# Attention and squared-ReLU FFN: softmax sums of four head pairs in one group, their inverse spread by DMAs from 16 rows

## The chip, the cores and the metric

The kernel runs on one core of one Trainium2 chip. The metric is device time in microseconds. Three runs of the kernel before took 481.18, 482.60 and 482.84 us, median 482.6.

The core has engines that work side by side, each with its own queue of instructions: TensorE (PE; PEld is its weight load), VectorE (DVE), ScalarE (ACT), GpSimd (POOL) and SyncE (SP). The last two only issue DMAs here, apart from some set-up on GpSimd. An instruction that waits holds up what is behind it on its own engine.

## The reference

Linear attention with projected keys and values, and then a feed-forward layer with a squared ReLU:

```python
k_proj = np.einsum('ks,bhsd->bhkd', E, k)
v_proj = np.einsum('ks,bhsd->bhkd', F, v)
scores = scale * np.matmul(q, k_proj.transpose(0, 1, 3, 2))
scores = scores - np.max(scores, axis=-1, keepdims=True)
attn = np.exp(scores)
attn = attn / (np.sum(attn, axis=-1, keepdims=True) + 1e-09)
attn_out = np.matmul(attn, v_proj)
x = attn_out.transpose(0, 2, 1, 3).reshape(B * S, H * D)
h = np.maximum(x @ w_in, 0.0)
out = h * h @ w_out
```

There are 8 batches (B), 8 heads (H), 1024 tokens (S) of 64 values (D), 64 projected keys, 512 columns in x, 2048 in h.

## The kernel before, in words

**Units.** A batch's attention is one `Attention` object. Its eight heads are four pairs, `pr` 0 to 3. The feed-forward layer of a batch is cut into two `Chunk`s of 512 tokens. After a start on plain products, both products of the layer use a seven-product scheme on 2x2 blocks (Strassen's, with sums of blocks formed on VectorE): `Group.p1` to `p7` for the first product, `second_spread` for the second. `sum_x` forms the block sums of x, four VectorE operations each.

**Attention of one batch, as steps of the plan.**
- `load_kv` and `load_q` bring K, V and Q from HBM by DMAs that GpSimd issues and that cast to bf16. Each of the three has one buffer, so the next batch's K and V wait for `project` to have read this one's.
- `project` multiplies K and V by E and F on TensorE; VectorE and ScalarE copy the result out of PSUM. `transpose_k_dma` and `transpose_q_dma` transpose by DMA, issued on SP.
- `scores(pr)` is four 64x64 matmuls into a PSUM tile `ps_att` of two banks, then one Exp on ScalarE into a tile `expT` (four buffers).
- `sums_spread(pr)` serves two pairs. Eight matmuls with a 64x32 block of ones put the sum of every token into 32 equal rows of `ps_att`, for each of four (pair, head) places. ScalarE makes the inverse as Exp(-Ln(sum)) in `inv`. SP then issues eight DMAs, each from 32 rows to 32 rows of a tile `rs`, so that every head has its inverse on all 64 rows. `inv` and `rs` share three buffers.
- `values(pr)` is four 64x64 matmuls from `expT` and the projected values into `ps_att`; two VectorE multiplications by `rs` (L409) write xT, the input of the feed-forward layer.

Batch 1 has another form, `sums(pr)`: the inverse is made twice by ScalarE, once for each pair, and four VectorE copies (L373) fill the missing rows.

**PSUM.** Up to batch 2's scores there are two `ps_att` tiles in turn (`turn["pairs"]`), from then on one. Every group of the attention therefore waits until the group before it has been read out. Four banks serve the first product, two the second.

**Order.** TensorE's order is that of the program, written by hand (`manual_schedule`). On the other engines a scheduler orders the instructions by its own simulation of when they become ready. The program is a generator: each `yield` is a step, and `plan` holds what `at(step, ...)` or `on(step, batch, name)` puts behind a step. In the steady part, `both()` takes in each step one block of the first product and mostly one block of the second, eight matmuls of 128x128 by 256 columns. A loop over b from 1 to 6 places, with t = 56 (b - 1), the attention of batches b + 1 and b + 2 among these steps; 56 steps are two chunks. For batch b + 2, `project` is at t + 30, `transpose_k_dma` at t + 32, the next K and V at t + 34, scores at 44, 47, 53 and, in the next period, 1; sums at 50 and 3; values at 7, 10, 20, 23 of the next period. In those steps, `second_spread` hands out an output (`put`) at steps 9, 21, 25, 29, 37, 49, 53 and 57 of the period. An output tile `o_sb` (three buffers) is stored by a DMA on SP. `keep` copies a partial product out of PSUM into a tile `u` (five buffers) that a later `relu_sum` (L666) or `put` adds.

The start differs: batch 0 runs in small pieces while the weights arrive, batch 1's attention lies among steps 36 to 60 of the next stretch, and batch 2's scores and first sums among the 16 steps of `chunk[1, 0].first_plain()`.

Of the kernel before, what the change touches and what calls it, by code (L numbers as in the profile page):

```python
# [9 lines left out]
P = 128  # L10
F32 = mybir.dt.float32
BF16 = mybir.dt.bfloat16
AF = mybir.ActivationFunctionType
# [6 lines left out]
def kernel(  # L20
# [43 lines left out]
    part_pool = ctx.enter_context(tc.tile_pool(name="part", bufs=5))  # L64
    out_pool = ctx.enter_context(tc.tile_pool(name="outp", bufs=3))
# [54 lines left out]
    nc.vector.memset(ones[:], 1.0)  # L120

# [100 lines left out]
    class Attention:  # L222
# [134 lines left out]
        def sums(self, pr):  # L357

            ps = att_psum()
            for j in range(2):  # L360
                for o, par, a, r in VALUE_QUADS:
                    c = 32 * (2 * a + j)
                    nc.tensor.matmul(
                        ps[c:c + 32, par], lhsT=ones[r, 0:32], rhs=self.e[pr + j][r, par], start=True, stop=True
                    )
            rs = [soft_pool.tile([P, 2, TCH], F32, tag="rs", name="rs") for _ in range(2)]
            nc.scalar.activation(rs[1][:], ps[:], AF.Ln)
            nc.scalar.activation(rs[0][:], rs[1][:], AF.Exp, scale=-1.0)
            nc.scalar.activation(rs[1][:], rs[1][:], AF.Exp, scale=-1.0)
            for j in range(2):  # L370
                for a in range(2):
                    have, lack = 32 * (2 * a + j), 32 * (2 * a + 1 - j)
                    nc.vector.tensor_copy(rs[j][lack:lack + 32], rs[j][have:have + 32])  # L373
                self.rs[pr + j] = rs[j]

        def sums_spread(self, pr):

            ps = att_psum()
            for j in range(2):
                for o, par, a, r in VALUE_QUADS:  # L380
                    c = 32 * (2 * a + j)
                    nc.tensor.matmul(
                        ps[c:c + 32, par], lhsT=ones[r, 0:32], rhs=self.e[pr + j][r, par], start=True, stop=True
                    )
            inv = soft_pool.tile([P, 2, TCH], F32, tag="rs", name="inv")
            nc.scalar.activation(inv[:], ps[:], AF.Ln)
            nc.scalar.activation(inv[:], inv[:], AF.Exp, scale=-1.0)
            for j in range(2):
                rs = soft_pool.tile([P, 2, TCH], F32, tag="rs", name="rs")
                for a in range(2):  # L390
                    have = 32 * (2 * a + j)
                    for to in (64 * a, 64 * a + 32):
                        nc.sync.dma_start(rs[to:to + 32], inv[have:have + 32])
                self.rs[pr + j] = rs
# [43 lines left out]
    class Chunk:  # L438
# [103 lines left out]
        def keep(self, ps):  # L542
            u = part_pool.tile([P, DM], F32, name="u")
            nc.scalar.copy(u[:], ps)  # L544
            return u
# [97 lines left out]
    class Group:  # L643
# [35 lines left out]
        def p5(self):  # L679
            self.other = bank(n=turn["bank"] + 2)  # L680
            self.product(5, self.other, True)
            self.kept5 = self.chunk.keep(self.other[:])

        def p6(self):
            self.product(6, self.chain)
            self.u2 = self.chunk.keep(self.chain[:])
# [21 lines left out]
    with tc.manual_schedule(engines={PE}):  # L708
# [81 lines left out]
        at(45, nxt.sums, 0)  # L790
        at(47, nxt.scores, 2)
        at(49, nxt.scores, 3)
        at(50, nxt.values, 0)
        at(52, nxt.values, 1)
        at(53, nxt.sums, 2)
# [11 lines left out]
        at(1, nxt.transpose_k)  # L807
        at(3, nxt.scores, 0)
        at(5, nxt.scores, 1)
        at(7, nxt.sums_spread, 0)  # L810
        at(9, nxt.scores, 2)
        at(11, nxt.scores, 3)
        turn["pairs"] = 1
        run_all(chunk[1, 0].first_plain())
# [45 lines left out]
        def on(step, b, name, *args):  # L860
            at(step, lambda: getattr(atts[b], name)(*args))

        for b in range(1, B - 1):
            t = 56 * (b - 1)
            if b > 1:
                on(t + 1, b + 1, "scores", 3)
            on(t + 3, b + 1, "sums_spread", 2)
            on(t + 7, b + 1, "values", 0)
            on(t + 10, b + 1, "values", 1)
            on(t + 20, b + 1, "values", 2)  # L870
            on(t + 23, b + 1, "values", 3)
            for c in range(2):
                at(t + 24, lambda b=b, c=c: chunk[b + 1, c].sum_x())
            if b + 2 < B:
                on(t + 2, b + 2, "transpose_q_dma")
                if b + 3 < B:
                    at(t + 2, begin, b + 3)
                    on(t + 3, b + 3, "load_q")
                on(t + 30, b + 2, "project")
                on(t + 32, b + 2, "transpose_k_dma")  # L880
                if b + 3 < B:
                    on(t + 34, b + 3, "load_kv")
                on(t + 44, b + 2, "scores", 0)
                on(t + 47, b + 2, "scores", 1)
                on(t + 50, b + 2, "sums_spread", 0)
                on(t + 53, b + 2, "scores", 2)
# [34 lines left out]
```

## Time and profile before

| what | value |
|---|---|
| median of three runs | 482.6 us |
| profiled execution, its own time | 482.35 us |
| span of the instructions in it | 480.5 us |
| TensorE busy | 470.4 us (98%) |
| VectorE busy | 350.7 us (73%) |
| ScalarE busy | 287.2 us (60%) |
| DMA of `rs` from `inv` on SP | 96 of 128 KB |
| small matmuls of `sums_spread` (L382) | 96, 4.9 us busy |
| Ln and Exp of `sums_spread` (L386, L387) | 12 each, 12.3 and 12.8 us busy |
| multiplications of `values` (L409) | 56, 36.0 us busy, 684 ns each |
| K and V, 1024 KB each in SBUF, issue to landing (median) | 9.5 and 15.8 us |

The profile is of one execution, whose span starts with its first instruction. Times in it are in microseconds unless ns is given. "Busy" is the union of an engine's instructions. A group line names the source line, the engine, the operation, what it writes and reads, the shapes and the count; behind the bar come busy time, mean ns of one, and the idle time of the engine just before, with what ended it. In a timeline, the first two columns are start and duration; brackets give the idle time before and what ended it. "issue" is time in which the engine waited for nothing that the profile shows. In the page's strips each digit is a fortieth of the span, in tenths.

### The profile page before, as it was taken

The numbers are of one execution on the slowest core, as the hardware profiler recorded it, in microseconds if no ns is written. First come the engines' busy times: TensorE is split into PE (matmuls) and PEld (weight loads), VectorE is DVE, ScalarE is ACT, GpSimd is POOL, SyncE is SP. The second block draws the span as 40 slices with busy tenths as digits, with TensorE's granted clock in tenths as the row PEclk, the third lists the DMA queues.
The fourth block names the chain that finished last, engine by engine and source line by source line (L and its number), as shares of the span: only waits on it lengthen the run. The fifth ranks groups of instructions, "written<-read, shape, count | busy, mean of one in ns | idle before, by whom it ended". The sixth has DMA issues, their size and how long they took to land.

```text
span 480.5 us, 10027 instructions
## 1 busy us (share of the span) xinstructions
PE 470.4 (98%) x4106; PEld 351.5 (73%) x4106; DVE 350.7 (73%) x613; ACT 287.2 (60%) x466; POOL 32.4 (7%) x45
## 2 busy tenths in 40 slices
PE   8999999999999999999999999999999999999996
PEld 3444445537878788787878778887887778888885
DVE  2456897956996679767897579966797678967671
ACT  2464467397547774678546785477745775565641
POOL 7310010200010000100010000100000000000000
PEclk9999999999999999999999999999999999999999
DMA  9999998999949496767939499495811054101012
GB/s 184 204 205 206 221 164 150 168 230 189 197 86 168 122 201 163 119 134 186 196 103 182 93 220 175 96 160 139 203 56 55 23 132 111 67 23 67 24 65 89
DMA packets 80046, 66.98 MB, mean 139 GB/s; under 512 B 30720, under 2 KB 76032, under 8 KB 80000
## 3 DMA queue, kind: packets, MB, share of 16 engines
q0 software_dynamic: 30640, 29.23, 39.4%
q1 hardware_dynamic: 49216, 36.97, 29.2%
q8 instruction: 32, 0.52, 0.4%
q10 hardware_dynamic: 144, 0.13, 0.1%
q14 instruction: 14, 0.11, 0.1%
HBM read 59.24 MB, written 16.78 MB: 158 GB/s over the span
## 4 chain that ended last, share of the span: by engine, by line
PE 71%; DVE 22%; ACT 3%; issue 2%; DMA 1%; DVEq 0%; ACTq 0%
PE ps_bank L652 28%; PE ps_second L572 27%; PE ps_bank L489 6%; DVE h L150 3%; DVE x_sum L150 3%; DVE h L666 3%; DVE s L150 2%; PE ps_att L329 2%; DVE xT L409 2%; PE ps_second L549 2%; PE ps_att L405 2%; DVE kp L246 1%; DVE rs L373 1%; DVE kp L247 1%; DVE w_in_sum L150 1%
## 5 line engine op out<-in xcount | busy, mean ns | idle before, releaser
L150 DVE TENSOR_TENSOR h<-h 128x1024 bf16<-128x1024 bf16 (+1 forms) x182 | 108.0, 616 | 39.1 <-ACT h L662 25.4
L652 PE MATMUL ps_bank<-x_sum,w_in_sum 128*128 128x256 bf16 x624 | 93.9, 273 | 0.0
L652 PEld LDWEIGHTS <-w_in_sum 128*128 128x128 bf16 x832 | 78.7, 98 | 16.2 <-issue 7.5
L572 PEld LDWEIGHTS <-h 128*128 128x128 bf16 x832 | 80.8, 98 | 10.6 <-DVE h L150 0.2
L662 ACT ACTIVATE h<-ps_bank 128x512 bf16<-128x512 f32 x104 | 62.9, 605 | 28.5 <-PE ps_bank L652 28.3
L544 ACT COPY u<-ps_bank 128x512 f32<-128x512 f32 x107 | 63.2, 591 | 26.6 <-PE ps_bank L652 23.6
L666 DVE CUSTOM_DVE_ANT_0 h<-ps_bank,u 128x512 bf16<-128x512 f32 x104 | 68.9, 685 | 13.0 <-PE ps_bank L652 12.5
L652 PEld LDWEIGHTS <-w_in 128*128 128x128 bf16 x624 | 58.8, 98 | 16.2 <-issue 9.5
L677 ACT COPY ps_bank<-ps_bank 128x512 f32<-128x512 f32 x52 | 29.7, 570 | 66.1 <-PE ps_bank L652 66.1
L572 PEld LDWEIGHTS <-s 128*128 128x128 bf16 x624 | 61.0, 98 | 7.1
L652 PE MATMUL ps_bank<-xT,w_in 128*128 128x256 bf16 x416 | 62.5, 273 | 0.0
L572 PE MATMUL ps_second<-w_out_sum,s 128*128 128x256 bf16 x416 | 62.4, 273 | 0.0
L572 PE MATMUL ps_second<-w_out_sum,h 128*128 128x256 bf16 x416 | 62.2, 273 | 0.0
L572 PE MATMUL ps_second<-w_out,h 128*128 128x256 bf16 x416 | 60.3, 273 | 0.0
L409 DVE TENSOR_TENSOR xT<-ps_att,rs 128x512 bf16<-128x512 f32 x56 | 36.0, 684 | 15.9 <-PE ps_att L405 15.9
L489 PE MATMUL ps_bank<-xT,w_in 128*128 128x512 bf16 x192 | 45.3, 379 | 1.8 <-DVE xT L434 1.0
L485 ACT ACTIVATE h<-ps_bank 128x512 bf16<-128x512 f32 x48 | 28.1, 606 | 16.1 <-PE ps_bank L489 15.9
L150 DVE TENSOR_TENSOR o_sb<-ps_second,u 128x512 f32<-128x512 f32 x27 | 18.5, 684 | 25.9 <-PE ps_second L572 20.7
L489 PEld LDWEIGHTS <-w_in 128*128 128x128 bf16 x192 | 17.7, 98 | 24.6 <-issue 6.2
L343 ACT ACTIVATE expT<-ps_att 128x1024 bf16<-128x1024 f32 x32 | 32.9, 1036 | 2.9 <-PE ps_att L329 2.5
L652 PE MATMUL ps_bank<-x_sum,w_in 128*128 128x256 bf16 x208 | 31.4, 273 | 1.4 <-DVE h L666 1.4
L652 PE MATMUL ps_bank<-xT,w_in_sum 128*128 128x256 bf16 x208 | 31.3, 273 | 0.0
(104 smaller groups left out, 477.2 us busy)
## 6 DMA issues: line engine op xcount, KB each, us to landing
out_dram<-o_sb SPq DMA_DIRECT2D x63, 256.0 KB, 2.4
rs<-inv SPq DMA_DIRECT2D x96, 128.0 KB, 2.8
K_sb<-in_k_dram POOLq DMA_DIRECT2D x7, 1024.0 KB, 9.5
V_sb<-in_v_dram POOLq DMA_DIRECT2D x7, 1024.0 KB, 15.8
Q_sb<-in_q_dram POOLq DMA_DIRECT2D x7, 1024.0 KB, 12.6
w_out<-in_moe_w_out_dram POOLq DMA_DIRECT2D x4, 512.0 KB, 17.9
w_in<-in_moe_w_in_dram POOLq DMA_DIRECT2D x3, 512.0 KB, 15.0
k_f<-in_k_dram SPq DMA_DIRECT2D x1, 512.0 KB, 4.9
```

The source lines that it names most:

```text
L150: return nc.vector.tensor_tensor(out=o, in0=x, in1=y, op=op)
L329: nc.tensor.matmul(ps[o, par], lhsT=self.kT[r, h % 4, h // 4, :], rhs=self.qT[r, h, n, :], start=True, stop=True)
L343: nc.scalar.activation(e[:], ps[:], AF.Exp, scale=SCALE)
L409: nc.vector.tensor_tensor(out=self.xT[:, pr, :, par], in0=ps_x[par].rearrange("p (c t) -> p c t", c=2), in1=rs[:, par].rearrange("p (c t) ...
L485: nc.scalar.activation(h, ps.rearrange("p (a t) -> p a t", a=2), AF.Relu)
L489: nc.tensor.matmul(ps[:], lhsT=w_in_blk(cb, fb), rhs=self.xT[:, cb, self.c].rearrange("p a t -> p (a t)"), start=(cb == 0), stop=(cb == NC ...
L544: nc.scalar.copy(u[:], ps)
L572: nc.tensor.matmul(ps[:, i * HM:(i + 1) * HM], lhsT=self.h_form(n, fb)[:, i * P:(i + 1) * P], rhs=w_out_form(n, fb), start=fresh and i == ...
L652: nc.tensor.matmul(ps[:, j * HC:(j + 1) * HC], lhsT=w_in_form(n, cb, 2 * self.g + j), rhs=self.chunk.x_form(n, cb), start=fresh and j == 0 ...
L662: nc.scalar.activation(self.out(kh, a), ps[:], AF.Relu)
L666: nc.vector._custom_dve(TENSOR_ADD_SAT, out=self.out(kh, a), in0=ps[:], in1=more[:], s0=3.0e38, s1=0.0)
L677: nc.scalar.copy(self.chain[:], self.first[:])
```

## The change

- `sums_all` replaces the two `sums_spread` of a batch, from batch 2 on. Sixteen matmuls accumulate in two rounds, m = 0 and 1, into one `ps_att`. Their weights are `pick`: 32 columns, of which 16 are ones and 16 zeros, so that pair 2m + j lands in 16 rows of a 32-row block and the other round adds zeros there. There is one Ln and one Exp for four pairs (`inverse_of`), in a tile `inv` with a buffer of its own.
- `spread` issues four DMAs for a pair, each from 16 rows to 64: a source row is read four times. All 16 DMAs of a batch are placed behind the sums, in one step. Four `rs` tiles share three buffers, `inv` is no longer among them.
- Batch 1's first sums (`sums(0, True)`) use the same DMAs instead of a second Exp and four copies; its second sums keep their form. Its later steps move by one.
- Batch 2's `transpose_k` and first two scores move one step later; its sums come at step 13 of `first_plain` instead of 7 and, for the second half, step 3 of the steady part.
- In the steady part `project` moves from 30 to 49 (24 for batch 3), with the transposition and the next K and V a step behind it; scores to 37, 40, 43, 46; all sums and spreads to 53; values to 6, 9, 19, 22 of the next period (7, 10, 19, 22 for batch 2); `sum_x` to 23 and 33 instead of twice 24; `transpose_q_dma` from 2 to 12, `load_q` from 3 to 26.
- The tiles of `keep` have two buffers for the first product and two for the second instead of five in common, `o_sb` has two instead of three.

```diff
-    part_pool = ctx.enter_context(tc.tile_pool(name="part", bufs=5))
-    out_pool = ctx.enter_context(tc.tile_pool(name="outp", bufs=3))
+    part_pool = ctx.enter_context(tc.tile_pool(name="part", bufs=2))
+    out_pool = ctx.enter_context(tc.tile_pool(name="outp", bufs=2))
...
+    pick = const_pool.tile([P, 2, 32], BF16, name="pick")
+    nc.vector.memset(pick[:], 0.0)
+    for m in range(2):
+        nc.vector.memset(pick[:, m, 16 * m:16 * m + 16], 1.0)
...
+            if by_dma:
+                self.inverse_of(ps)
+                for j in range(2):
+                    self.spread_rows(pr + j, {(par, a): (32 * (2 * a + j), par) for o, par, a, r in VALUE_QUADS})
+                return
...
+        def sums_all(self):
+            ps = att_psum()
+            for m in range(2):
+                for j in range(2):
+                    for o, par, a, r in VALUE_QUADS:
+                        c = 32 * (2 * j + par)
+                        nc.tensor.matmul(
+                            ps[c:c + 32, 0 if r == LO else 1], lhsT=pick[r, m], rhs=self.e[2 * m + j][r, par],
+                            start=m == 0, stop=m == 1, skip_group_check=True,
+                        )
+            self.inverse_of(ps)
+
+        def inverse_of(self, ps):
+            self.inv = soft_pool.tile([P, 2, TCH], F32, tag="inv", name="inv", bufs=1)
+            nc.scalar.activation(self.inv[:], ps[:], AF.Ln)
+            nc.scalar.activation(self.inv[:], self.inv[:], AF.Exp, scale=-1.0)
+
+        def spread(self, pr):
+            m, j = divmod(pr, 2)
+            self.spread_rows(pr, {
+                (par, a): (32 * (2 * j + par) + 16 * m, 0 if r == LO else 1) for o, par, a, r in VALUE_QUADS
+            })
+
+        def spread_rows(self, pr, at):
+            rs = soft_pool.tile([P, 2, TCH], F32, tag="rs", name="rs")
+            for o, par, a, r in VALUE_QUADS:
+                row, n = at[par, a]
+                nc.sync.dma_start(rs[o, par], self.inv[row:row + 16, n].unsqueeze(1).broadcast_to((16, 4, TCH)))
+            self.rs[pr] = rs
...
-        def keep(self, ps):
-            u = part_pool.tile([P, DM], F32, name="u")
+        def keep(self, ps, tag="second"):
+            u = part_pool.tile([P, DM], F32, name="u", tag=tag)
...
-        at(45, nxt.sums, 0)
...
+        at(45, nxt.sums, 0, True)
...
-        at(7, nxt.sums_spread, 0)
...
+        on(13, 2, "sums_all")
+        for pr in range(4):
+            on(13, 2, "spread", pr)
...
+        def project(step, b):
+            on(step, b, "project")
+            on(step + 1, b, "transpose_k_dma")
+            if b + 1 < B:
+                at(step + 1, begin, b + 1)
+                on(step + 1, b + 1, "load_kv")
+
+        project(24, 3)
         for b in range(1, B - 1):
             t = 56 * (b - 1)
...
-            on(t + 7, b + 1, "values", 0)
-            on(t + 10, b + 1, "values", 1)
-            on(t + 20, b + 1, "values", 2)
-            on(t + 23, b + 1, "values", 3)
+            for pr, step in enumerate((7, 10, 19, 22) if b == 1 else (6, 9, 19, 22)):
+                on(t + step, b + 1, "values", pr)
             for c in range(2):
-                at(t + 24, lambda b=b, c=c: chunk[b + 1, c].sum_x())
+                at(t + 23 + 10 * c, lambda b=b, c=c: chunk[b + 1, c].sum_x())
             if b + 2 < B:
-                on(t + 2, b + 2, "transpose_q_dma")
+                on(t + 12, b + 2, "transpose_q_dma")
                 if b + 3 < B:
-                    at(t + 2, begin, b + 3)
-                    on(t + 3, b + 3, "load_q")
-                on(t + 30, b + 2, "project")
-                on(t + 32, b + 2, "transpose_k_dma")
-                if b + 3 < B:
-                    on(t + 34, b + 3, "load_kv")
-                on(t + 44, b + 2, "scores", 0)
-                on(t + 47, b + 2, "scores", 1)
-                on(t + 50, b + 2, "sums_spread", 0)
-                on(t + 53, b + 2, "scores", 2)
+                    on(t + 26, b + 3, "load_q")
+                    project(t + 49, b + 3)
+                for pr in range(4):
+                    on(t + 37 + 3 * pr, b + 2, "scores", pr)
+                on(t + 53, b + 2, "sums_all")
+                for pr in range(4):
+                    on(t + 53, b + 2, "spread", pr)
```

## The prediction

> **What bounds the kernel now.** I read the page first, then busy time by period, the waits of TensorE, and the timeline around one group of softmax sums.
>
> ```profile
> span 480.5 us, 10027 instructions
> ...
> PE 470.4 (98%) x4106; PEld 351.5 (73%) x4106; DVE 350.7 (73%) x613; ACT 287.2 (60%) x466; POOL 32.4 (7%) x45
> ...
> DMA  9999998999949496767939499495811054101012
> ```
>
> TensorE is busy for 98% of the span. The middle of the program repeats with the 56-step period of the plan; the first columns below are the stretch, its length and PE's busy time:
>
> ```profile
> 220.50:276.40 55.90, 55.62 (x514) 44.77 (x512) 43.47 (x74) 35.83 (x60) 2.62 (x3) 1.00 0.76 154
> ```
>
> So a period costs what TensorE's own work costs, about 55.85 us. Its only wait on an engine there comes once a period, five times in all:
>
> ```profile
> PE ps_bank L652 <- DVE h L666: 1.4, 5, 0.3
> ```
>
> ```profile
> 144.62 0.69 DVE L666 CUSTOM_DVE_ANT_0 h<-ps_bank,u 128x512 bf16<-128x512 f32 x1
> ...
> 145.37 0.31 PEld L652 LDWEIGHTS <-w_in 128*128 128x128 bf16 x3 [0.46 <-issue]
> ```
>
> VectorE comes late there because the copies of `project` (steps 30 on) and both `sum_x` (step 24) meet. That costs 0.45 us a period. Anything that makes TensorE wait is therefore added to the end, and only TensorE's own work or this 0.45 can be gained. One group of sums before the change:
>
> ```profile
> 380.55 0.60 PE L572 MATMUL ps_second<-w_out,s 128*128 128x256 bf16 x4
> 381.08 0.11 PEld L382 LDWEIGHTS <-ones 64*32 64x32 bf16 x8 [0.21 <-issue]
> 381.08 0.41 PE L382 MATMUL ps_att<-expT,ones 64*32 64x512 bf16 x8
> 381.42 0.33 PEld L652 LDWEIGHTS <-w_in_sum 128*128 128x128 bf16 x4 [0.23 <-issue]
> ...
> 382.95 1.07 ACT L387 ACTIVATE inv<-inv 128x1024 f32<-128x1024 f32 x1
> ...
> 384.04 5.84 SPq L393 DMA_DIRECT2D rs<-inv  x8
> ...
> 394.25 0.41 PE L405 MATMUL ps_att<-expT,vp 64*64 64x512 bf16 x4
> ```
>
> From 380.55 to 381.42 is 0.87 us; four ordinary matmuls account for 0.436 (381.87 to 382.74 holds two such blocks, one step of 0.872). So the eight small matmuls cost TensorE 0.437 us. They run together: the next weight load follows 0.34 after their start. The inverse is ready 2.94 us after the sums start, and `values(0)` comes 13.17 us after them. What a spread DMA takes depends on what else flows. Three windows (103 to 108.3 us, beside the K and V loads; 175.5 to 179, beside a Q load; 384 to 390, beside no load), last column the median us to landing:
>
> ```profile
> rs<-inv SPq DMA_DIRECT2D x8, 128.0 KB, 6.4
> ```
> ```profile
> rs<-inv SPq DMA_DIRECT2D x4, 128.0 KB, 7.8
> ```
> ```profile
> rs<-inv SPq DMA_DIRECT2D x8, 128.0 KB, 2.4
> ```
>
> The third is hidden work today, and so are the other two: 13 to 17 steps lie between a group of sums and the values that use it.
>
> [...] eight 64x32 matmuls together, with 0.21 and 0.23 us of "issue" on either side. [...] The source falls from 32 rows to 16[...]. No trace of before has a 16-row source.
>
> **The change, part by part.** S is the start of `sums_all`; a step is 0.872 us, an attention group of one 64-row burst 0.437.
>
> *Sums at once.* Sixteen matmuls instead of twice eight: [...] 0.65 against 0.87: 0.22 less, for batches 2 to 7 (six): -1.3 us. [...] I take -1.3. ScalarE loses one Ln and one Exp (1.02 + 1.06) a batch, worth nothing: TensorE covers it.
>
> *`project` to step 49, one `sum_x` to 33.* The 0.45 us wait loses its cause: 5 x 0.45 = -2.2 us (0 if the casts now meet other work). Between `project` and `sums_all` lie four steps, 3.5 us, for 4 x 0.41 + 0.69 us of copies: 1.1 to spare. Costs nothing; without that spare, up to 1 us a batch.
>
> *Scores to steps 37 to 46.* Four groups, three steps (2.6 us) apart as before, one Exp of 1.04 between: nothing.
>
> *The spread meets the next load.* This is the large term. Before, `load_kv` followed `project` at step 30; the transfers ran some 16.6 us and were over before the sums of step 50 spread (328 and 384 us: 2.3 to 3.6 us a DMA). Now `project` ends 3.5 us before S and K, V of the following batch start there: they flow to about S+13. With the inverse at S+3.2 and SP issuing every 0.63 us, the fourth DMA goes out at S+5.1 and lands 7.4 later, at S+12.5. `values(0)` is now only nine steps away: 9 x 0.872 + 0.65 = S+8.5, its VectorE products due at S+9.0. They wait 3.5 us, and in VectorE's queue the `relu_sum`s and squares wait behind them. They end at S+13.9 (2 x 0.684). `values(1)` is due at S+11.55 and needs the same single `ps_att` buffer, so TensorE stands 2.3 us. The second pair's last DMA goes out at S+7.6 and lands at S+15.0, 0.6 after its shifted due time[...]. I take 3.0 us a batch (1.5 to 5). It concerns the sums that a load follows: batches 3, 4, 5: +9.0. Batches 6 and 7 have no load: [...] +0.3 together (0 to 2). Batch 2's sums (step 13) end with their load almost over: +0.3.
>
> *Batch 1 by DMA.* ScalarE saves one Exp (1.06), VectorE four copies (2.7), neither on the path. Eight DMAs are added on SP. The sums start at 70.77, the inverse is there about 73.6, the fourth DMA goes out at 75.5, while V (to 75.1) and Q (70.3 to 80.6) flow: it lands near 83.0, products end at 84.4. `sums(2)`, now step 54, about 82.2, needs that PSUM pair: +2.2 us (0 to 3.5). Moving this group's steps by one costs nothing: same work.
>
> *Smaller pools.* `out_pool` has two buffers. Of the four outputs of the first batch's second chunk, the second's store goes out at 87.95 and lands at 96.35; the fourth, copied by ScalarE at 92.65, has had a third buffer and now waits 3.7 us. Behind it stand the `vp` cast and the relus that free TensorE's banks; some 2.2 us of banks cover: +1.5 (0 to 3). In the steady part a buffer comes round after two outputs, 3.5 us or more against 2.4 to landing: nothing[...]. The keeps' two buffers "first" need the last `relu_sum` done before the next `p5` copy: 1.6 to 4.7 us apart now, so nothing by itself; it makes a late VectorE felt sooner. `pick`'s memsets (0.1 us each) hide at the start before E arrives. Moving `transpose_q_dma` to step 12 and `load_q` to 26 puts them behind the spreads on SP, with the next scores at step 37: nothing; uncovered, the transposition and its issue are some 7 us.
>
> **Sum.** -1.3 - 2.2 + 9.0 + 0.3 + 0.3 + 2.2 + 1.5 = +9.8 us. The span 480.5 becomes 490.3; 1.85 us lie around it in the profiled execution (482.35), so 492.2, and the median of the runs stands 0.25 higher: 492.4, say 492.
>
> **Rivals.**
> *The spreads arrive in time* (faster): only the two gains stay, 482.6 - 3.5 = 479.1. It decides at one point: the first pair's DMAs must land by S+10.2, i.e. within about 5 us of issue beside the load. For it: 2.4 us without a load. Against: medians of 6.4 and 7.8 with one, and K and V start by the plan itself just before. 0.13.
> *Gains and waits cancel* (within 0.5%, which is about what a measurement of this kernel can tell from no change: 480.2 to 485): VectorE's slack takes the lateness, only one or two batches stall, say 3.5 us of waits: 482.6. For it: slack of up to 4.7 us. Against: `ps_att` is one buffer. 0.13.
> *The 16-row source is the bound*: [...] stores queued behind on SP, outputs waiting for two buffers. Some 3.5 us in each of six batches beside the early losses: 482.6 - 3.5 + 21 + 3.7 = 504. 0.07.
>
> **How the numbers follow.** The forecast has 0.67 and its own range of 485 to 500. The whole range, 480.5 to 500, leaves out the fast rival and the heavy one, 0.2. Faster 0.13, same 0.13, slower 0.74.
>
> **What would show it.** Right: products L409's counterpart waiting for DMA landings of `rs`, in the periods of batches 3 to 5 but hardly later; the spread's median to landing at 6 us or more there; TensorE waiting on VectorE just before the second `values`; a first-output ScalarE wait near 93 us. The sums' burst of 16 at 0.65 us and the end of the 0.45 us wait show the gains. Wrong: periods of 55.2 us throughout, or the same lateness with and without loads, which would point to the source rows.

## The result, and the profile after

The kernel after takes 508.9 us (median of four runs, 505.5 to 510.82); the kernel before took 481.89 beside it (median of four). The ratio is 1.0552, with a 95% interval of 1.0488 to 1.0615: slower, and by more than twice what was forecast. The profiled execution took 508.01 us, with a span of 506.2, which is 25.7 more than before.

From the page of the kernel after:

```profile
span 506.2 us, 10077 instructions
...
PE 475.1 (94%) x4106; PEld 355.8 (70%) x4106; DVE 348.3 (69%) x612; ACT 275.8 (54%) x453; POOL 32.5 (6%) x45
...
PEclk9999998999899999999899998999999999999999
DMA  9999999999769899209981399614682038401012
```

TensorE has the same 4106 matmuls. It is idle for 21 us more than before (31.1 against 10.1), and it is busy for 4.7 us longer. The strip of the granted clock says why it is busy for longer: four slices show an 8. The clock's own record has five stretches of 3.4 us at half clock (0.50 of full, as the trace has it), starting at 83.0, 130.8, 188.8, 250.2 and 311.7 (the third falls on two slices and doesn't show); before, there was none until the last 0.1 us of the span.

The waits of TensorE after, by what it waited for (total us, times, longest):

```profile
PE ps_att L426 <- DVE xT L430: 11.5, 3, 4.3
PE ps_bank L673 <- DVE h L687: 4.9, 4, 4.2
PE ps_att L367 <- DVE xT L430: 2.3, 1, 2.3
PE ps_bank L510 <- ACT o_sb L583: 2.3, 1, 2.3
```

L426 is `values`, L430 its products on VectorE, L687 `relu_sum`, L367 batch 1's `sums(2)`. Each of the first line's three waits lies in one of the periods of batches 3, 4 and 5 (3.8, 3.3 and 4.3 us, ending at 189.25, 249.40 and 310.82); batches 6 and 7 have none.

**The lateness, block by block.** Since both kernels run the same blocks of the feed-forward layer in the same order, the same matmul can be looked up in both traces. How late the kernel after is, worked out from the two start times:

| block in the kernel before, us | in the kernel after, us | late by | added since the row above |
|---|---|---|---|
| 53.7 | 52.8 | -0.9 | |
| 111.4 | 115.7 | 4.3 | 5.2 (batch 1, first outputs) |
| 167.2 | 179.6 | 12.3 | 8.1 (batch 2; one `project` more, about 1.9, is already done) |
| 223.1 | 240.2 | 17.1 | 4.8 (batch 3) |
| 278.9 | 300.6 | 21.7 | 4.6 (batch 4) |
| 334.8 | 362.1 | 27.3 | 5.6 (batch 5) |
| 390.6 | 415.5 | 24.9 | -2.4 (batch 6; it no longer contains a `project`) |

The two windows of the kernel after that begin at 240.2 and 362.1 (stretch, length, PE, PEld, DVE, ACT and POOL busy, then clock, DMA share, GB/s):

```profile
240.20:300.60 60.40, 56.90 (x514) 45.80 (x513) 43.47 (x74) 34.02 (x58) 2.62 (x3) 0.97 0.72 144
362.10:415.50 53.40, 53.39 (x499) 44.15 (x497) 41.14 (x69) 33.45 (x57) 0.00 (x0) 1.00 0.43 80
```

Where a load follows, a period takes 60.4 us against 55.9, at a mean clock of 0.97. Where none does, TensorE is never idle. That period, corrected for the missing `project` (the gap between the kernels shrinks by 1.9 us where only the kernel before projects, 184.3 to 195.5 of its trace), is 0.5 us shorter than before.

TensorE's last matmul ends 24.9 us later than before (501.65 against 476.77). The other 0.8 us of the 25.7 lie behind it, in the last copy of an output, here before and after:

```profile
477.26 0.42 DVE L560 COPY o_sb<-ps_second 128x256 f32<-128x256 f32 x1 [1.50 <-ACT o_sb L562]
```
```profile
502.98 0.42 DVE L581 COPY o_sb<-ps_second 128x256 f32<-128x256 f32 x1 [2.29 <-DMA out_dram<-o_sb]
```

It starts 0.5 us behind the last matmul before and 1.3 behind it after, where the trace names the store of an earlier output: `o_sb` has one buffer less. No run gave that buffer back.

**One late batch.** For batch 3, SP's queue:

```profile
165.71 4.89 SPq L325 DMA_TRANSPOSE qT<-Q_sb  x1
...
176.94 20.77 SPq L414 DMA_DIRECT2D rs<-inv  x16
```

and the timeline from 184 to 192, beside the four matmuls of an ordinary block:

```profile
186.95 0.69 DVE L430 TENSOR_TENSOR xT<-ps_att,rs 128x512 bf16<-128x512 f32 x1 [3.80 <-DMA rs<-inv]
...
188.51 0.69 DVE L430 TENSOR_TENSOR xT<-ps_att,rs 128x512 bf16<-128x512 f32 x1 [0.87 <-DMA rs<-inv]
...
189.25 0.64 PE L426 MATMUL ps_att<-expT,vp 64*64 64x512 bf16 x4 [3.83 <-DVE xT L430]
...
189.85 1.01 PE L673 MATMUL ps_bank<-x_sum,w_in 128*128 128x256 bf16 x4
```

S, the start of `sums_all`, is 173.76, and the inverse is ready at 176.92. The first spread DMA lands 9.1 us after its issue, the fourth, issued at 180.25, at 188.41, which is S+14.65. `values(0)` has long been there (S+8.1), so VectorE's queue stands for 3.80 us (first line; the next `relu_sum` in it starts at 189.12, behind both products), and `values(1)` cannot have the PSUM pair. K, V and Q of the next batch were issued at 170.53, 171.39 and 172.98 and landed at 183.81, 192.40 and 200.37. The last line is the second cost: four matmuls that take 0.60 us elsewhere take 1.01 here, at half clock.

What a spread takes beside that load (177 to 198), and without one (359 to 377, batch 6), last column the median us to landing:

```profile
rs<-inv SPq DMA_DIRECT2D x16, 128.0 KB, 8.1
```
```profile
rs<-inv SPq DMA_DIRECT2D x16, 128.0 KB, 4.8
```

**The gain.** The burst of sixteen, alone in TensorE's timeline:

```profile
355.73 0.60 PE L593 MATMUL ps_second<-w_out,s 128*128 128x256 bf16 x4
356.25 0.63 PE L393 MATMUL ps_att<-expT,pick 64*32 64x512 bf16 x16
356.81 0.61 PE L673 MATMUL ps_bank<-xT,w_in 128*128 128x256 bf16 x4
```

From 355.73 to 356.81 is 1.08 us, less 0.436 for the four ordinary matmuls: 0.645, where the forecast had 0.65, an estimate.

### The profile page after: what moved, and what is told of

The parts are those of the page before. It is cut to its first block, busy times and chain, and to the rows that moved or that the text cites. A ratio compares the mean times of both kernels' runs of the same rounds, so it can differ in the third digit from the quotient of the medians.

```text
span 506.2 us, 10077 instructions
## 1 busy us (share of the span) xinstructions
PE 475.1 (94%) x4106; PEld 355.8 (70%) x4106; DVE 348.3 (69%) x612; ACT 275.8 (54%) x453; POOL 32.5 (6%) x45
## 4 chain that ended last, share of the span: by engine, by line
PE 63%; DMA 21%; DVE 6%; ACT 4%; SPq 2%; issue 1%; POOL 1%; DVEq 0%; ACTq 0%; POOLq 0%
PE ps_bank L673 27%; PE ps_second L593 26%; DMA rs<-inv 8%; DMA out_dram<-o_sb 6%; DMA w_out<-in_moe_w_out_dram 4%; DMA V_sb<-in_v_dram 3%; PE ps_bank L510 3%; SPq L414 2%; PE ps_att L262 2%; PE ps_att L333 2%; PE ps_second L570 1%; PE ps_bank L570 1%; PE ps_att L426 1%; DVE w_out_sum L154 1%; DVE h L154 1%
## 5 line engine op out<-in xcount | busy, mean ns | idle before, releaser
L673 PE MATMUL ps_bank<-x_sum,w_in_sum 128*128 128x256 bf16 x624 | 95.4, 276 | 4.6 <-DVE h L687 4.5
L673 PEld LDWEIGHTS <-w_in_sum 128*128 128x128 bf16 x832 | 79.9, 99 | 21.8 <-issue 12.2
L683 ACT ACTIVATE h<-ps_bank 128x512 bf16<-128x512 f32 x104 | 62.2, 598 | 31.6 <-PE ps_bank L673 30.2
L687 DVE CUSTOM_DVE_ANT_0 h<-ps_bank,u 128x512 bf16<-128x512 f32 x104 | 69.2, 685 | 8.4 <-PE ps_bank L673 6.9
L673 PEld LDWEIGHTS <-w_in 128*128 128x128 bf16 x624 | 59.9, 99 | 15.5 <-issue 8.1
L593 PEld LDWEIGHTS <-s 128*128 128x128 bf16 x624 | 62.5, 100 | 8.5
L430 DVE TENSOR_TENSOR xT<-ps_att,rs 128x512 bf16<-128x512 f32 x56 | 37.2, 687 | 41.4 <-DMA rs<-inv 41.0
L593 PE MATMUL ps_second<-w_out_sum,s 128*128 128x256 bf16 x416 | 65.3, 281 | 0.0
L510 PEld LDWEIGHTS <-w_in 128*128 128x128 bf16 x192 | 17.8, 97 | 26.9 <-issue 8.2
L506 ACT ACTIVATE h<-ps_bank 128x512 bf16<-128x512 f32 x48 | 27.6, 601 | 15.5 <-PE ps_bank L510 15.4
L673 PE MATMUL ps_bank<-x_sum,w_in 128*128 128x256 bf16 x208 | 32.6, 281 | 0.4 <-DVE h L687 0.4
L593 PE MATMUL ps_second<-w_out,s 128*128 128x256 bf16 x208 | 31.2, 273 | 0.0
```

Source lines behind the costliest of these rows:

```text
L430: nc.vector.tensor_tensor(out=self.xT[:, pr, :, par], in0=ps_x[par].rearrange("p (c t) -> p c t", c=2), in1=rs[:, par].rearrange("p (c t) ...
L506: nc.scalar.activation(h, ps.rearrange("p (a t) -> p a t", a=2), AF.Relu)
L510: nc.tensor.matmul(ps[:], lhsT=w_in_blk(cb, fb), rhs=self.xT[:, cb, self.c].rearrange("p a t -> p (a t)"), start=(cb == 0), stop=(cb == NC ...
L593: nc.tensor.matmul(ps[:, i * HM:(i + 1) * HM], lhsT=self.h_form(n, fb)[:, i * P:(i + 1) * P], rhs=w_out_form(n, fb), start=fresh and i == ...
L673: nc.tensor.matmul(ps[:, j * HC:(j + 1) * HC], lhsT=w_in_form(n, cb, 2 * self.g + j), rhs=self.chunk.x_form(n, cb), start=fresh and j == 0 ...
L683: nc.scalar.activation(self.out(kh, a), ps[:], AF.Relu)
```

## The experiments

The theory: in batches 3 to 5 the spreads are late because they flow beside the loads of K, V and Q (A in the expectations); batches 1 and 2 and the outputs of batch 0 each add a wait of their own. The rival (B) is the source: 16 rows would be too slow, load or not. The third one, formed during the work (C), is a wait for the buffer of `inv`. All ratios are to the kernel before on the same chip, medians of four or more runs except where stated.

### No loads after the fourth batch

```diff
         def load_kv(self):
+            if self.b > 3:
+                self.K, self.V = atts[3].K, atts[3].V
+                return
...
         def load_q(self):
+            if self.b > 3:
+                self.Q = atts[3].Q
+                return
```

> The changed kernel without the loads of K, V and Q of batches 4 to 7; these batches compute with batch 3's K, V and Q, so this work is left out. Theory A (the spread DMAs are late because K, V and Q flow at the same time): the four waits of 4.2, 3.8, 3.3 and 4.3 us in the periods of batches 2 to 5 go, and with them four stretches of half clock at 1.7 us each, 22.4 us in all; the time falls from about 508.9 to 486.5, and no spread takes over 6 us after 116 us. Theory B (the 16-row source alone makes them late): the waits stay, at least 10 us of them, and the time stays above 500.

489.69 us, ratio 1.0165 (1.0144 to 1.0186). All lateness of batches 3 to 5 and its half clock are gone. TensorE's waits are now:

```profile
PE ps_att L432 <- DVE xT L436: 4.0, 1, 4.0
PE ps_att L373 <- DVE xT L436: 2.1, 1, 2.1
PE ps_bank L679 <- DVE h L693: 1.3, 4, 0.5
```

The second is batch 1. The first is batch 2, ending at 123.5; I had expected it to go too, and the time is 3.2 us above the expected 486.5. Batch 2's inverse was ready at 111.0, but SP was held by the transposition of Q(3), issued beside the load of V(3), which landed at 114.09:

```profile
106.10 9.26 SPq L331 DMA_TRANSPOSE qT<-Q_sb  x1
115.46 10.69 SPq L420 DMA_DIRECT2D rs<-inv  x10
```

So the load is what makes batches 3 to 5 late, and batch 2 is a case of its own.

### The loads of K and V alone

The same, with only `load_q` changed, so that K and V still flow.

> The changed kernel without the loads of Q of batches 4 to 7 alone (they use batch 3's Q, so this work is left out); K and V are loaded. If K and V alone make the spreads late by what I forecast, the waits of batches 3 to 5 are 2 to 3 us each instead of 3.3 to 4.3, and 3 to 8 us are gained: 501 to 506. If Q's load, which joins them, makes most of the lateness, the waits fall under 1.5 us, the half clocks go, and the time is below 497. If Q adds nothing: within 1.5 us of 508.9.

504.9 us, 1.0469 (1.0436 to 1.0503). The waits of batches 3 to 5 are 2.9, 3.7 and 2.3 us, against 3.8, 3.3 and 4.3 with Q; the half-clock stretches stay. K and V make most of the lateness; Q, whose load I had not counted, adds about 0.8 us a batch (11.4 less 8.9, over three). The 8.9 us with K and V alone are what the forecast had for just these loads, 9.0.

### The old 32-row spreads in the new schedule

```diff
         def spread(self, pr):
-            m, j = divmod(pr, 2)
-            self.spread_rows(pr, {
-                (par, a): (32 * (2 * j + par) + 16 * m, 0 if r == LO else 1) for o, par, a, r in VALUE_QUADS
-            })
+            rs = soft_pool.tile([P, 2, TCH], F32, tag="rs", name="rs")
+            for a in range(2):
+                have = 32 * (2 * a + pr % 2)
+                for to in (64 * a, 64 * a + 32):
+                    nc.sync.dma_start(rs[to:to + 32], self.inv[have:have + 32])
+            self.rs[pr] = rs
...
```

`sums_all` is here one burst of eight with the old block of ones.

> The changed kernel at its own steps, with the 16 DMAs of a batch in the old form, 32 rows to 32. Pairs 2 and 3 are given the inverses of pairs 0 and 1, so half of the sums' matmuls (0.2 us a batch) are left out. If K, V and Q in flight alone make the spreads late, the waits of 3.8, 3.3 and 4.3 us in the periods of batches 3 to 5 shrink by under 1 us each and the time stays at 502 or above. If the 16-row source is needed for it, they fall under 1.5 us, their half clocks go, and the time is about 495 or below. Batches 6 and 7 have no wait either way.

503.54 us, 1.0451 (1.0425 to 1.0477). TensorE still waits for the same products, 5.1, 3.0 and 4.7 us in batches 3 to 5, and there are four half-clock stretches, three of them 6.8 us long:

```profile
PE ps_att L426 <- DVE xT L430: 16.1, 5, 5.2
```

In batch 3 the first spread lands 10.1 us after its issue and the fourth at S+15.2, no earlier than from 16 rows (S+14.65). The source is not needed for the lateness. The run is 5.4 us faster all the same, but the difference lies ahead of batch 2's period: at the block of 111.4 us in the kernel before, the kernel after is 4.3 late and this one not at all. From there to the block of 390.6 this one loses more, 22.2 us against 20.6.

What the source costs by itself shows without a load. Batch 6 of the kernel after spreads sixteen DMAs in 20.97 us (359.44 to 380.41), 1.3 us each, with 4.8 to landing; in this run batch 6 spreads sixteen in 12.40 us (357.01 to 369.41), 0.78 each:

```profile
rs<-inv SPq DMA_DIRECT2D x16, 128.0 KB, 2.3
```

### The 16-row source in the old schedule

```diff
-                for a in range(2):
+                for o, par, a, r in VALUE_QUADS:
                     have = 32 * (2 * a + j)
-                    for to in (64 * a, 64 * a + 32):
-                        nc.sync.dma_start(rs[to:to + 32], inv[have:have + 32])
+                    nc.sync.dma_start(rs[o, par], inv[have:have + 16, par].unsqueeze(1).broadcast_to((16, 4, TCH)))
```

> The kernel before, with only its 96 spread DMAs in the new form, 16 rows read four times into 64. Theory A: 13 to 17 steps lie between sums and values, so the time stays within 1 us of before, 481 to 483, although the eight DMAs of a group take about 10 us instead of 7.7. Theory B: TensorE waits for late values as in the changed kernel, at least 5 us in all, 487 or more.

509.18 us, 1.0573 (1.0548 to 1.0598): a clear miss. No product of `values` is late. In the timeline, SP's spread of the first two pairs, then the Ln of the second two and TensorE:

```profile
162.06 5.87 SPq L392 DMA_DIRECT2D rs<-inv  x8
...
171.64 1.02 ACT L386 ACTIVATE inv<-ps_att 128x1024 f32<-128x1024 f32 x1 [2.83 <-PE ps_bank L651]
...
173.19 0.60 PE L651 MATMUL ps_bank<-x_sum,w_in_sum 128*128 128x256 bf16 x4 [2.19 <-ACT u L543]
```

The sums that this Ln reads began at 168.29. The name in its brackets, an L651 long done, isn't what held it. By the code the second `inv` takes the buffer of the first, three turns on, and must wait until all eight DMAs have read it; the last of them lands at 171.41, 0.23 us before the Ln. In the kernel before the eight were done in some 7.75 us after their first issue; here it took 9.35. Ln, and with it every copy queued behind it on ScalarE, is late, and TensorE waits about 3.4 us a period; four half-clock stretches come on top.

### The same with the first sums three steps earlier

To give the DMAs that time: `project` at 27 instead of 30, and everything up to `sums_spread(0)` likewise.

```diff
-                on(t + 50, b + 2, "sums_spread", 0)
+                on(t + 47, b + 2, "sums_spread", 0)
...
```

> The kernel before with 16-row spreads (as in e2) and, in the steady part, project, its transposition, the next K and V, scores 0 and 1 and the first sums three steps earlier (27, 29, 31, 41, 44, 47). Theory C (in e2 nothing is late for the values; the first group's eight 16-row DMAs end 1.6 us later, and the second group's Ln, which overwrites the same inv buffer, waits for them on ScalarE, and TensorE behind it): 2.6 us more between the two groups remove that wait in batches 3 to 7 and the time falls from 509.2 to 481 to 486. Theory B (16-row spreads themselves slow the whole kernel, by late values or by the traffic they make): it stays above 500.

494.67 us, 1.0249 (1.023 to 1.0269). That is 14.5 us less than the run before it, and no half clock is left, as theory C has it for most of the loss. (The direct test, an `inv` with a buffer of its own in the old schedule, was not run.) It does not reach the expected 481 to 486: 1.7 us a period remain, 0.8 behind the copy of `ps_second` on ScalarE and 0.85 behind VectorE (L150), where the moved `project` meets the block sums, and 2.7 us in batch 2, whose sums the edit doesn't move. The 16-row source thus can cost as much as the whole change, but by another way, and one that the kernel after, where `inv` has its own buffer and one user a batch, doesn't have.

### Batch 1 with its old sums

```diff
-        at(45, nxt.sums, 0, True)
+        at(45, nxt.sums, 0)
```

> The changed kernel with batch 1's first sums in the old form (a second Exp and four copies, no DMA). Theory A: the wait of 2.3 us at 82.3 us and its half clock of 1.7 go, 4.0 us less, about 504.9. Theory B says the same for this group if its eight DMAs were late; a rival, that ScalarE's and VectorE's added work costs what the DMAs cost, leaves the time within 1 us of 508.9.

506.66 us, 1.0514 (1.0487 to 1.0541). The wait at 82 us and its half clock are gone, as expected, 4 us together; but the time falls by 2.2 only. Batch 2's wait has grown from 4.2 to 5.6, and two half-clock stretches are now 6.8 us long.

### Batch 0's later outputs in another pool

```diff
-            o = out_pool.tile([P, 2, HM], F32, name="o_sb")
+            if self.b == 0 and a != mh:
+                o = part_pool.tile([P, 2, HM], F32, name="o_sb", tag="first")
+            else:
+                o = out_pool.tile([P, 2, HM], F32, name="o_sb")
```

> The changed kernel with the third and fourth output of the first batch's second chunk in two buffers that are idle then (those of the keeps named first). Theory A: ScalarE's wait of 10.4 us for an output buffer goes, and with it TensorE's waits of 2.2 and 0.8 us near 98 and 101 us: 3.0 less, about 505.9. Rival (the wait has cover, and the time comes back at the next group): within 1 us of 508.9.

In the kernel after, one output copy stands 10.4 us on ScalarE:

```profile
97.92 0.59 ACT L583 COPY o_sb<-ps_bank 128x512 f32<-128x512 f32 x1 [10.37 <-DMA out_dram<-o_sb]
```

With the tile apart, this wait and TensorE's 2.3 and 0.8 us behind it are gone, and the time is 509.17 us, 1.0559 (1.0526 to 1.0593): the same. Batch 2's wait grew from 4.2 to 6.3 and three half-clock stretches became 6.8 us long. TensorE reached batch 2's values earlier, the DMAs did not: they stood on SP behind the transposition of Q(3), which here took 10.10 us (105.81 to 115.91).

### The block sums apart, in the kernel before

```diff
-                at(t + 24, lambda b=b, c=c: chunk[b + 1, c].sum_x())
+                at(t + 24 + 14 * c, lambda b=b, c=c: chunk[b + 1, c].sum_x())
```

> The kernel before with the second sum_x at step 38 instead of 24, nothing else. If the wait of 0.45 us in each period comes from VectorE having both sum_x and project's copies before the relu_sum, it goes in five periods: 2.2 us less, about 479.3. If it comes from project's copies alone, within 0.5 us of before.

481.95 us against 482.42, ratio 0.9991 (0.9981 to 1.0001): no gain that can be told. The wait of 0.45 behind `relu_sum` is gone, and one of 0.42 behind ScalarE's copy of `ps_second` stands in its place.

### Holding TensorE, in the kernel before

ScalarE copies `expT` onto itself n = 0 to 4 times behind the first scores of a period, and four extra matmuls on TensorE must wait for it.

```diff
+        def hold(self, pr, n):
+            ps = att_psum()
+            for _ in range(n):
+                nc.scalar.copy(self.e[pr][:], self.e[pr][:])
+            for o, par, a, r in VALUE_QUADS:
+                c = 64 * a
+                nc.tensor.matmul(
+                    ps[c:c + 32, par], lhsT=ones[r, 0:32], rhs=self.e[pr][r, par], start=True, stop=True
+                )
...
+                on(t + 44, b + 2, "hold", 0, b - 1)
```

> The kernel before with one wait of TensorE put into each of five periods, right behind scores 0: four small matmuls that wait for the Exp of these scores and for 0, 1, 2, 3 and 4 copies of 1.04 us of its result onto itself. TensorE stands for about 1.5 to 2 us and 1 us more in each period. If idle time itself brings the half clock, the record of the granted clock shows 0.5 for 3.4 us behind the holds of about 2.3 us and more (the changed kernel: a wait of 2.3 with it, one of 2.2 without) and none behind the first; each costs 1.7 us beside the wait. If the half clock has another cause (traffic, the late spreads), it does not appear at all.

One run, 504.96 us. TensorE waits 1.13, 2.20, 3.28, 4.36 and 5.43 us, and the half clock follows only the last two, for 6.8 us from 330.9 and 3.4 from 395.8. No DMA is late here: idle time of 4.36 and 5.43 us was enough. Yet a wait of 3.28 did not bring it here (first line), and one of 2.33 did in the kernel after (second line):

```profile
271.29 0.40 PE L402 MATMUL ps_att<-expT,ones 64*32 64x512 bf16 x4 [3.28 <-ACT expT L399]
```
```profile
82.31 0.41 PE L367 MATMUL ps_att<-expT,ones 64*32 64x512 bf16 x8 [2.33 <-DVE xT L430]
```

The last section sets such waits beside the times at which the stretches start.

### Values later

```diff
-            for pr, step in enumerate((7, 10, 19, 22) if b == 1 else (6, 9, 19, 22)):
+            for pr, step in enumerate((13, 16, 19, 22)):
```

> The changed kernel with the values of each batch at steps 13, 16, 19, 22 instead of 6 (7), 9 (10), 19, 22. The first pair then has 16 steps (14.6 us) behind the sums; in the changed kernel it landed 14.7 us behind them and the second 20.2. If the distance is what fails, the waits of batches 2 to 5 (4.2, 3.8, 3.3, 4.3) fall to 1 to 2 us and most of their half clocks go: 490 to 499. If lateness comes from SP or ScalarE being held up elsewhere, the waits move with the values, and the time stays above 504.

504.92 us, 1.048 (1.0459 to 1.0502). The waits of batches 3 to 5 for late values fall to 0.8 to 1.2 us; batch 2's is still 2.5. In exchange all products and the block sums now stand close together before the blocks that need them:

```profile
PE ps_bank L673 <- DVE h L687: 8.4, 12, 2.4
```

with 1.9 to 2.4 us at 205.7, 265.1 and 324.4. The lateness moved from the DMAs to VectorE; 4 us are gained of some 27.

### Sums and spreads 11 steps earlier

A try at a version better than both: batches 1 and 2 and the outputs as in the kernels above that repaired them, scores from step 30, `sums_all` and the spreads of two pairs at 42, the others at 58 and 63.

```diff
-                    on(t + 37 + 3 * pr, b + 2, "scores", pr)
-                on(t + 53, b + 2, "sums_all")
-                for pr in range(4):
-                    on(t + 53, b + 2, "spread", pr)
+                    on(t + 30 + 3 * pr, b + 2, "scores", pr)
+                on(t + 42, b + 2, "sums_all")
+                for pr, step in enumerate((42, 42, 58, 63)):
+                    on(t + step, b + 2, "spread", pr)
...
```

> Sums of four pairs at once, kept from the change, with room: batches 1 and 2 as before, scores from batch 3 on at steps 30, 33, 36, 39, all sums at 42, the spreads of pairs 0 and 1 there and of 2 and 3 at 58 and 63, project(3) at 14, the four outputs as in e4. 20 steps then lie between sums and the first values. If time is all that the spreads lack, no wait of TensorE above 0.5 us is left from batch 3 on, no half clock, and the time is 479 to 482, at or just under before. If the 16-row spreads cost time in other ways (SP held up before the stores, output buffers), 484 to 492.

494.91 us, 1.0267 (1.024 to 1.0293). No values are late. A new wait has come, on ScalarE:

```profile
ACT o_sb L603 <- DMA out_dram<-o_sb: 24.7, 9, 5.1
```

The stores stand on SP behind the spreads, which take 8 us to land, and with two output buffers ScalarE stands too; TensorE waits 1.9, 2.4 and 2.9 us behind it. It is not better than the kernel before.

### All causes taken out at once

The kernel after without the late loads, with batch 1's and batch 2's old sums and the outputs apart. The diff is that of the pieces above, and:

```diff
-        on(13, 2, "sums_all")
-        for pr in range(4):
-            on(13, 2, "spread", pr)
...
+        at(7, nxt.sums_spread, 0)
...
+        on(3, 2, "sums_spread", 2)
         project(24, 3)
```

> The kernel after without the loads of K, V and Q of batches 4 to 7 (these batches compute with batch 3's data: the loads are left out), with batch 1's first sums and batch 2's sums in their old forms and places and with two of batch 0's outputs in another pool. If the load beside the spreads, batch 1, batch 2 and the output wait, with the half-clock stretches they bring, are all there is to the loss, then nothing of it is left, and what the change gains remains: about 0.5 us in each of five periods. 479.5 us (477.5 to 481.5), no TensorE wait of more than 0.6 us after 60 us, no half-clock stretch. If the 16-row source or the sums of four pairs cost something of their own in the steady part, 485 us or more, with VectorE's products late by over 2 us in batches 3 to 7.

483.14 us, ratio 1.0024 (1.0013 to 1.0035). No TensorE wait after 60 us is longer than 0.7, and no half-clock stretch lies behind the start. The sums of four pairs at once and the 16-row spreads are still in this kernel for batches 3 to 7, and a period takes

```profile
281.30:336.90 55.60, 55.47 (x514) 44.95 (x513) 43.37 (x74) 34.13 (x58) 0.00 (x0) 1.00 0.52 98
```

55.60 us, where the kernel before took 55.90 for the same blocks. So the named causes, taken together, are nearly all of the loss, and the gain is about 0.3 us a period, not the 0.67 of the forecast. That the total stays 3.6 above the expected 479.5 has three parts. The block that starts at 96.9 us before starts at 98.3 here; a half-clock stretch at 7.5 us and waits of 0.6 and 0.7 near 79 and 95 us lie ahead of it, and weren't followed further. From there to TensorE's last matmul the run gains 1.3 us, where the expectation had 2.5. And behind the last matmul stand the 0.8 us of the kernel after (4.57 us to the end of the span, 3.76 before).

## Why the prediction was wrong in size

The direction and the main mechanism were right: `values(1)` waits behind products that wait for `rs` beside the next load, in batches 3 to 5 and not in 6 and 7; `sums(2)` of batch 1 waits 2.3 us (2.2 forecast); ScalarE's output wait near 93 us is there. 492.0 was forecast, with a range to 500; it is 508.9. The step that failed most is the way the sum was made: each wait of TensorE was booked at its own length, and the half clock that follows it, 8.0 us in all, at nothing. Next to it stands batch 2, booked at 0.3 us and measured at 4.7. Step by step, for the profiled execution:

| step of the sum | forecast, us | measured, us |
|---|---|---|
| sums at once | -1.3 | -1.3 (0.645 a burst) |
| the 0.45 wait | -2.2 | about -1, an estimate; none when made alone |
| batches 3 to 5, spreads beside the load | +9.0 | +11.4 (3.8, 3.3, 4.3) |
| batches 6 and 7 | +0.3 | 0 |
| batch 2 | +0.3 | +4.2, and 0.5 at the next scores |
| batch 1 | +2.2 | +2.3, less 0.4 of a wait that it takes the place of |
| outputs of batch 0 | +1.5 | +3.0 (2.3 and 0.8) |
| half clock | not in it | +8.0 |
| sum | +9.8 | +26.7 |

This execution was 0.9 us ahead at 53.7 us, and the last output copy, which the forecast had at nothing, adds 0.8. That makes 26.6, where 25.7 were found. The surplus lies ahead of batch 2: there the terms give 6.6 us, with one half-clock stretch, and the table of blocks 5.2. It wasn't followed further.

- **The term that was missing is the half clock.** Five stretches of 3.4 us lose 1.7 each, 8.5 in all; TensorE was idle anyway for 1.1 us of them, so 0.5 comes off. The forecast took a wait to cost its own length. In the other three runs of the kernel after the mean granted clock was 0.986, 0.973 and 0.970 (0.983 in the profiled one), and the times rise as it falls: 505.5, 509.8, 510.8 us. The forecast didn't look at the granted clock at all.
- **"Batch 2's sums (step 13) end with their load almost over: +0.3"** failed. V(3) was indeed in at 110.49. But the transposition of Q(3) went out before the spreads, at 109.04, which frees the one Q buffer, and Q(4) was loaded from 117.58 to 131.96, across the second pair's DMAs:

```profile
109.04 4.71 SPq L325 DMA_TRANSPOSE qT<-Q_sb  x1
113.96 17.44 SPq L414 DMA_DIRECT2D rs<-inv  x16
```

  The second pair landed at 128.97, and `relu_sum`, queued behind its products, let TensorE go at 131.47. Without the late loads of Q the wait is still 2.85, and without K, V and Q it is 4.0. There Q(4) does not flow, but the transposition itself holds SP longer, 8.1 and 9.3 us, as long as V(3) is still being loaded (it lands at 112.4 and 114.1). So two causes stand in for each other. No run took both away with the new sums of batch 2 kept.
- **"Moving `transpose_q_dma` to step 12 and `load_q` to 26 puts them behind the spreads on SP ... nothing"** failed for the same reason. The order in the program is not SP's order: the scheduler puts a transposition out when what it needs is there. Here that was the one buffer of qT, which the last scores of batch 3 free. With all four scores moved ahead of the sums, these end at 165.66, and the transposition went out at 165.71:

```profile
165.25 0.41 PE L333 MATMUL ps_att<-qT,kT 64*64 64x512 bf16 x4
```

  In the kernel before, the last scores came at step 1 of the next period, behind the first sums. So the transposition now went ahead of the spreads, and Q's load, which I had placed after them, joined those of K and V. Q took 27.4 us to land, and "K, V flow to about S+13" became S+18.6 for V and S+26.6 for Q.
- **The size of the lateness.** I took 7.4 us to landing for the fourth DMA, from the windows of before; it was 8.2, and the issue came 1.4 later than forecast (S+6.5). The 3.0 was mis-sized by 0.8, which is what Q's load adds by the run without it.
- **The 0.45 us wait** was treated as if nothing stood behind it. There was another 0.42 us behind ScalarE. With all causes out, the kernel gains 1.3 us from 111.4 us to the last matmul, hardly more than the shorter bursts of five batches (5 x 0.22).
- **Outputs.** 3.0 against 1.5 is within what was bounded, but taking it away alone gave nothing.

The rival of the 16-row source came nearest in number (504), yet for a reason that the runs refute: the lateness is there with 32 rows, and not in batches 6 and 7. How much slower a 16-row DMA would be was only an estimate of mine; without a load it took 1.3 us, and one from 32 rows 0.78.

## What to carry to other kernels

Work out for a moved transfer which loads will flow at its new place, and for every buffer that a moved transfer frees, which load that starts; a hand-written order is not that of a queue which a scheduler fills. In the kernel after, five of TensorE's six waits of 2.3 us or more were followed by a half-clock stretch that cost 1.7 us: in a kernel like this one, book a long wait with that chance on top. Repairing one of several late transfers first gives its time to the next one: here the outputs' wait, batch 1 and the late loads gave 0, 2 and 19 us when taken away alone, and 26 together with batch 2's old sums.

## What the runs showed that I had not expected

**When the half clock came.** By the clock's record of the kernel after, each of the five half-clock stretches is 3.413 us long, and from the start at 83.0 those at 130.8, 188.8, 250.2 and 311.7 are 14, 31, 49 and 67 times this length. In the run with the holds, the starts at 330.9 and 395.8 are 19 such lengths apart. So TensorE's idle time can be summed in each window of that grid. In the kernel after, the five windows at full clock just ahead of the stretches have 2.33, 3.41, 3.37, 2.77 and 2.75 us of idle; of those behind 45 us that full clock followed, the two with the most have 1.93 (from 96.6) and 1.76 (from 304.9). The same sums over the clock records of all ten profiled executions that have such stretches: 57 windows at full clock after 45 us have 1.2 us of idle or more; none of the 20 with up to 1.87 us was followed by half clock, all 33 with 2.0 or more were, and of four between 1.88 and 1.93, two were. Of the 45 windows at half clock in these executions, the 10 with 0.81 us of idle or more were followed by another, which makes the stretches of 6.8 us, and the 35 with up to 0.70 by full clock. The hold of 3.28 us lay across two windows of its run's grid, 1.45 and 1.83 us in each, and no half clock followed; the 2.33 us of the kernel after lay within one, and it did. In the first experiment a wait of 2.1 us, at 82.1, was followed by it too. The ends of matmuls are modelled in the trace, so these sums are approximate.

**A transposition's issue under load.** One transposition of Q holds SP for 4.7 to 5.0 us in the kernel after. Beside a load of V it took 9.26 us in the first experiment, 10.10 with the outputs apart, 8.84 with batch 1's old sums, 8.07 without the late Q and 6.46 in the kernel before, each ending 1.2 to 2.8 us after V had landed. What is queued behind it on SP waited as long: in the first experiment the transposition ended at 115.36, and the first spread behind it was issued at 115.46.
